# Gated attention and state-space kernel, forward and backward: head strips of 20 rows and single-bank exponentials in place of strips of 32 rows and two-bank exponentials

## The chip, the core and the metric

The kernel runs on one core of a Trainium2 chip. A core has a matmul engine (TensorE, PE in the profile, with its weight loads as PEld), a vector engine (DVE), an engine for activation functions (ACT), a general engine (GpSimd, POOL) and a queue for transfers (SyncE, SP). Sixteen DMA engines move data. Matmul results land in PSUM; the other working memory is SBUF. The metric is the device time of one execution, in microseconds: 3192.69 us before, the median of 3 runs from 3189.31 to 3194.74 us.

## The reference

Input x has 2048 rows of 576. One branch is attention with 32 heads of 18, the other a long convolution whose kernel is made from a diagonal state-space model (576 channels, 128 states); a gate mixes them. The outputs are the forward result and the gradients of all twelve trained inputs.

```python
qkv = (x @ wqkv).reshape(B, S, 3, H, Dh).transpose(2, 0, 3, 1, 4)      # S=2048, H=32, Dh=18
scores = einsum("bhqd,bhkd->bhqk", q, k) * Dh ** -0.5
o = einsum("bhqk,bhkd->bhqd", softmax(scores), v)
a = o.transpose(0, 2, 1, 3).reshape(B, S, D) @ wo
# the other branch
P = exp(dt * A * l);  K = real(einsum("dn,dnl,dn->dl", C, P, dt * Bc))    # complex A, B, C
b = causal_convolution(u, K) + u * Dskip                                 # written with FFTs
g = sigmoid((x * gate_w).sum(-1, keepdims=True))
out = g * a + (1 - g) * b
# outputs: out, and jax.vjp of it at grad_out
```

## The kernel before

The program has four parts in order: preparation, attention (forward and backward in one sweep), the convolution with its gradients, and a final part with the projections of the gradients.

**Preparation.** Loads and transposes x; makes a row-reversed copy of x; projects q, k and v per group of 7 heads, and stores each transposed, head by head, in memory. Each head has a strip of 32 rows: 18 of data, a row for the softmax bound or a constant, and 13 further rows, zeros. Four heads make 128 rows. The constant rows are written by GpSimd's queue out of a tile that uses the space of `x_pad`.

```python
QaT_d = dram.tile([NG, P, S], BF); KaT_d = ...; VaT_d = ...       # NG = 8 groups of 4 heads, P = 128
rows = [t_.rearrange("g (j w) s -> (g j) w s", w=HP) for t_ in (QaT_d, KaT_d, VaT_d)]   # HP = 32

def put_constants():
    con = s1.tile([P, 3, S // 4], BF, tag="xp")                      # the space of x_pad
    ...
    for a_ in range(4):
        for t_ in rows:
            nc.gpsimd.dma_start(t_[:, DH + 1:HP, sl], con[pt, 0:1, :].to_broadcast([H, HP - DH - 1, S // 4]))
        nc.gpsimd.dma_start(rows[1][:, DH, sl], con[pt, 2, :])        # -1
        nc.gpsimd.dma_start(rows[2][:, DH, sl], con[pt, 1, :])        # 1
...
for m, (h0, hn) in enumerate(hts):                                  # groups of 7 heads
    for which in (1, 0, 2):                                         # k, q, v
        for tb in range(NBK):
            for c, (d0, dsz) in enumerate(dch):                     # 576 = 4 x 128 + 64
                mm(ps[0:fn], lhsT=wqkv_sb[0:dsz, c, ...], rhs=xT[0:dsz, ...], ...)
            ...                                                     # eviction to stg, squares, row sums
        nc.sync.dma_start(rows[which][h0:h0 + hn, 0:DH, :], stg[0:fn, :])
...
for t in range(NT):                                                 # gradient of attention's output, through wo
    ... nc.sync.dma_start_transpose(out=d_aT, in_=d_a); nc.sync.dma_start(gyr_d[...], gy_b)   # each 4 tiles
    ... mm(psd, lhsT=d_aT[0:esz, ...], rhs=woT[0:esz, ...]); ... nc.sync.dma_start(dO_d[:, t, :], dO_t)
for r_, src_ap in enumerate((A_re, A_im, B_re, B_im, C_re, C_im)):   # parameters, two buffers
    for c, (d0, dsz) in enumerate(dch):
        nc.sync.dma_start(blk_[0:dsz, c, :], src_ap[d0:d0 + dsz, :])
    nc.sync.dma_start_transpose(out=pr_, in_=blk_)
... # powers of the poles on ACT and DVE, stored to par_d by SyncE
```

**Attention.** 32 units, each a group of 4 heads and 512 queries; a unit has 32 steps G. In a step two heads' scores (P1) are made for the forward side, two heads' scores of the transposed side (P3) and two heads' dP (P2) for a unit that runs 39 steps behind. A score matmul contracts over 32 rows of one strip, so matmuls of different strips run side by side on PE. A pair of score tiles lies in two PSUM banks, and one ACT instruction takes the exponential of both.

```python
NFILL = (0, 0, 1, 4)                       # filler matmuls by phase of four steps
def s_pair(kind):
    return apsp.tile([P, 2, KB], F32, tag="S", bufs=2)               # KB = 512
for G in range(NTOT + OFF + 24):
    ps = s_pair("P1")
    for x in range(2):
        row(ps[:, x, :], T["KaT"][:, i * P:(i + 1) * P], T["QaT", b], j0 + x)
    if G % 4 in (3, 0): ... 4 matmuls accO <- Vtok, PT                # the forward result
    ps = s_pair("P3")
    for x in range(2):
        row(ps[:, x, :], T["QaT", b][...], T["KaT"][...], jo + x)
    for x in range(2):
        row(ps_P2, T["VaT", ...], U["dOaT"], j2)                     # dP, two single banks
    ACC.append(accB(...)); fill(ACC[0], NFILL[ph])                    # one bank for dV, dQ, dK in turn
    ... # burst: 8 matmuls of dV, 8 of dQ, 16 of dK, or the fillers alone, one kind per step
    nc.scalar.activation(U["PT"][i][:, j:j + 2, :], ps, ACT.Exp)      # P1
    nc.scalar.activation(e, ps, ACT.Exp)                              # P3, e is [P, 2, KB]
    nc.vector.tensor_tensor(U["ds"][i][:, j, :], ps, U["PT"][i][:, j, :], op=A.mult)   # each of two P2
    ... # eviction of the burst on VectorE; DMA transpose of ds when 4 heads are there
```

PSUM's eight banks: two pairs of scores (4), dP (2), accO (1), accB (1). Pieces of the strips are loaded as 128-row tiles (`QaT`, `KaT`, `VaT`) and, transposed by DMA, as token tiles (`Vtok`, `Ktok`, `Qtok`). At the first steps of a unit the previous one's softmax normalisation is done: a copy of accO, four transposes on PE, then work on VectorE and GpSimd, and a DMA transpose to `dOaT`. Beside all this GpSimd computes powers of the poles (`E_d`) for the convolution.

Of the kernel before, what the change touches and what calls it, by code (L numbers as in the profile page):

```python
# [17 lines left out]
P = 128  # L18


def build(tc, aps, dbg_aps=None, stages=("s1", "attn", "post", "s4", "final")):
# [18 lines left out]
    H = 32  # L40
# [4 lines left out]
    assert DH + 2 <= HP  # L45
# [15 lines left out]
    with ExitStack() as gctx:  # L61
# [15 lines left out]
        QaT_d = dram.tile([NG, P, S], BF, name="QaT_d")  # L77
        KaT_d = dram.tile([NG, P, S], BF, name="KaT_d")
        VaT_d = dram.tile([NG, P, S], BF, name="VaT_d")
# [17 lines left out]
        dt_d = dram.tile([P, D], F32, name="dt_d")  # L97
        CB = 32
# [14 lines left out]
        with ExitStack() as ctx:  # L113
# [11 lines left out]
            x_pad = s1.tile([P, NT, DPAD], BF, tag="xp", name="x_pad")  # L125
            nc.gpsimd.memset(x_pad[:, :, D:DPAD], 0.0)
            wqkv_sb = s1.tile([P, DC, F], BF, name="wqkv_sb")
            xT = s1.tile([P, NT, DC, P], BF, name="xT")
# [20 lines left out]
            rows = [t_.rearrange("g (j w) s -> (g j) w s", w=HP) for t_ in (QaT_d, KaT_d, VaT_d)]  # L149
            xb_v = xb_d.rearrange("b (k r) w -> b k r w", r=XR)  # L150

            def put_constants():

                con = s1.tile([P, 3, S // 4], BF, tag="xp", name="con")
                for q_, v_ in enumerate((0.0, 1.0, -1.0)):
                    nc.gpsimd.memset(con[:, q_, :], v_)
                for a_ in range(4):
                    sl = slice(a_ * S // 4, (a_ + 1) * S // 4)
                    pt = slice(a_ * H, (a_ + 1) * H)
                    for t_ in rows:  # L160
                        nc.gpsimd.dma_start(t_[:, DH + 1:HP, sl], con[pt, 0:1, :].to_broadcast([H, HP - DH - 1, S // 4]))
                    nc.gpsimd.dma_start(rows[1][:, DH, sl], con[pt, 2, :])
                    nc.gpsimd.dma_start(rows[2][:, DH, sl], con[pt, 1, :])

            hsel = s1.tile([P, HT], BF, name="hsel")
            nc.gpsimd.memset(hsel, 1.0)
            nc.gpsimd.affine_select(out=hsel, in_=hsel, compare_op=A.is_ge, fill=0.0,
                                    base=0, pattern=[[-DH, HT]], channel_multiplier=1)
            nc.gpsimd.affine_select(out=hsel, in_=hsel, compare_op=A.is_ge, fill=0.0,
                                    base=DH - 1, pattern=[[DH, HT]], channel_multiplier=-1)  # L170

            for t in range(NT):
                xr_t = work.tile([P, D], BF, tag="xr_t4", bufs=4, name="xr_t4")
                for u in range(2):
                    psr = psB.tile([P, 512], F32, tag="dO", bufs=2, name="psr")
                    mm(psr[:, 0:DH2], lhsT=J_bf, rhs=x_pad[:, t, u * DH2:(u + 1) * DH2])
                    if u == 0:
                        nc.vector.tensor_copy(xr_t[:, 0:DH2], psr[:, 0:DH2])
                    else:
                        nc.scalar.copy(xr_t[:, DH2:D], psr[:, 0:DH2])  # L180
                nc.sync.dma_start(xr_d[:, t, :], xr_t)
# [9 lines left out]
            put_constants()  # L191
            kmx = s1.tile([HT, len(hts), NBK], F32, name="kmx")
            kmxg = s1.tile([HT, len(hts)], F32, name="kmxg")
            for m, (h0, hn) in enumerate(hts):
                fn = hn * DH
                for which in (1, 0, 2):
# [3 lines left out]
                    for tb in range(NBK):  # L200
                        ps = psA.tile([P, TB, P], F32, tag="proj", bufs=4, name="ps_proj")
                        for c, (d0, dsz) in enumerate(dch):
                            mm(ps[0:fn], lhsT=wqkv_sb[0:dsz, c, which * D + h0 * DH:which * D + h0 * DH + fn],
                               rhs=xT[0:dsz, tb * TB:(tb + 1) * TB, c, :], start=(c == 0), stop=(c == DC - 1))
# [12 lines left out]
                        ps2 = psB.tile([HT, TB * P], F32, tag="ps2", name="ps2")  # L217
                        mm(ps2[0:hn], lhsT=hsel[0:fn, 0:hn], rhs=sq[0:fn])
# [15 lines left out]
            for t in range(NT):  # L234
# [11 lines left out]
                for u, (f0, fsz) in enumerate(HALF):  # L246
                    psd = psB.tile([P, 512], F32, tag="dO", bufs=2, name="ps_dO")
                    for c, (e0, esz) in enumerate(dch):
                        mm(psd[:, 0:fsz], lhsT=d_aT[0:esz, t % TB, c, :], rhs=woT[0:esz, c, f0:f0 + fsz],
                           start=(c == 0), stop=(c == DC - 1))  # L250
# [12 lines left out]
            for r_, src_ap in enumerate((A_re, A_im, B_re, B_im, C_re, C_im)):  # L263
                blk_ = work.tile([P, DC, N], BF, tag="pblk", name="pblk")
                nc.vector.memset(blk_[:, DC - 1, :], 0.0)
                for c, (d0, dsz) in enumerate(dch):
                    nc.sync.dma_start(blk_[0:dsz, c, :], src_ap[d0:d0 + dsz, :])
# [64 lines left out]
        if "attn" in stages:  # L332
# [4 lines left out]
            NFILL = (0, 0, 1, 4)  # L337
            with ExitStack() as ctx:
# [15 lines left out]
                PB = {"QaT": 3, "VaT": 4, "Vtok": 5, "Ktok": 4, "Qtok": 2}  # L354

                def load_full(g):
                    t_ = ga.tile([P, S], BF, tag="KaT", bufs=2, name="KaT_g")
                    nc.sync.dma_start(t_, KaT_d[g])
                    grp_t.setdefault(g, {})["KaT"] = t_

                def load_piece(nm, g, m):
                    src = {"QaT": QaT_d, "VaT": VaT_d, "Vtok": VaT_d, "Ktok": KaT_d, "Qtok": QaT_d}[nm][g][:, m * KB:(m + 1) * KB]
                    if nm in ("QaT", "VaT"):
                        t_ = ga.tile([P, KB], BF, tag=nm, bufs=PB[nm], name=nm + "_g")
                        nc.sync.dma_start(t_, src)
                    else:
                        t_ = ga.tile([P, TPQ, 4, HP], BF, tag=nm, bufs=PB[nm], name=nm + "_g")
                        nc.sync.dma_start_transpose(out=t_.rearrange("p t h w -> p t (h w)"), in_=src)
# [64 lines left out]
                def row(ps, l, r, j):  # L433
                    r0 = HP * j
                    mm(ps, lhsT=l[r0:r0 + DA], rhs=r[r0:r0 + DA], tile_position=(r0, 0))

                def s_pair(kind):
                    return apsp.tile([P, 2, KB], F32, tag="S", bufs=2, name="ps_" + kind)
# [955 lines left out]
```

## Time and profile before

| | PE | DVE | ACT | POOL |
|---|---|---|---|---|
| busy, us | 2580.9 | 2389.7 | 2394.6 | 1803.1 |
| share of the span of 3191.0 us | 81% | 75% | 75% | 57% |

A share of the whole span mixes stages, so the table of stretches (busy time of each engine between two times) is read with it. A line of a group in the profile gives the line of the program, the engine, output and inputs with shapes, the number of instructions, then busy time in us and the mean of one in ns, then the idle time of the engine just ahead of them and what ended it. In the views by time, the first number is the start, the second the duration, and "x4" means four instructions merged in one line. A busy time counts overlapping instructions once; the durations of neighbours can overlap, so what an engine needs for one is read from start to start.

### The profile page before, as it was taken

The numbers are of one execution on the slowest core, as the hardware profiler recorded it, in microseconds if no ns is written. First come the engines' busy times: TensorE is split into PE (matmuls) and PEld (weight loads), VectorE is DVE, ScalarE is ACT, GpSimd is POOL, SyncE is SP. The second block draws the span as 40 slices with busy tenths as digits, with TensorE's granted clock in tenths as the row PEclk, the third lists the DMA queues.
The fourth block names the chain that finished last, engine by engine and source line by source line (L and its number), as shares of the span: only waits on it lengthen the run. The fifth ranks groups of instructions, "written<-read, shape, count | busy, mean of one in ns | idle before, by whom it ended". The sixth has DMA issues, their size and how long they took to land. (4 is left out here: it accounts for less than half of the span.)

```text
span 3191.0 us, 69289 instructions
## 1 busy us (share of the span) xinstructions
PE 2580.9 (81%) x26530; PEld 1162.4 (36%) x26530; DVE 2389.7 (75%) x4309; ACT 2394.6 (75%) x2760; POOL 1803.1 (57%) x3376
## 2 busy tenths in 40 slices
PE   6668888888888888888888888888856877885498
PEld 2222222222222222222222222222215777775255
DVE  4245787888788788888788878888855888888533
ACT  3239898998899899899899989998846676773010
POOL 1019888888888888888888888887010000000000
PEclk9778999999999899999899999999977888887799
DMA  8966999999999999999999999998898787862995
GB/s 224 152 166 113 182 174 186 176 172 175 182 167 171 186 165 180 185 178 174 177 186 171 178 187 171 173 184 164 148 186 219 207 207 200 213 176 65 278 241 131
DMA packets 1536483, 572.12 MB, mean 179 GB/s; under 512 B 1428511, under 2 KB 1503650, under 8 KB 1526934
## 3 DMA queue, kind: packets, MB, share of 16 engines
q1 hardware_dynamic: 1514278, 509.95, 81.9%
q0 software_dynamic: 21872, 57.74, 7.4%
q8 instruction: 207, 3.39, 0.4%
q14 instruction: 126, 1.03, 0.1%
HBM read 153.55 MB, written 102.83 MB: 80 GB/s over the span
## 5 line engine op out<-in xcount | busy, mean ns | idle before, releaser
L768 DVE TENSOR_TENSOR ds<-ps_P,PT 128x512 bf16<-128x512 f32 x2048 | 1316.0, 684 | 305.0 <-ACT eb L763 143.3
L758 ACT ACTIVATE PT<-ps_P 128x1024 bf16<-128x1024 f32 x1024 | 1064.6, 1042 | 171.4 <-PE ps_P L30 155.9
L763 ACT ACTIVATE eb<-ps_P 128x1024 bf16<-128x1024 f32 x1024 | 1072.7, 1048 | 28.4 <-PE ps_P L30 26.9
L542 POOL TENSOR_TENSOR et<-eG,eT 128x256 f32<-128x256 f32 x1152 | 700.7, 629 | 35.2
L30 PE MATMUL ps_P<-KaT_g,QaT_g 32*128 32x512 bf16 x2048 | 411.9, 391 | 102.8 <-ACT eb L763 98.2
L30 PE MATMUL ps_P<-dOaT,VaT_g 32*128 32x512 bf16 x2048 | 449.5, 395 | 23.1 <-DMA dOaT<-dOa 14.7
L542 POOL TENSOR_TENSOR Eo<-et,et 128x256 bf16<-128x256 f32 x576 | 418.7, 727 | 43.1
L30 PE MATMUL ps_P<-QaT_g,KaT_g 32*128 32x512 bf16 x2048 | 416.7, 404 | 20.6 <-DMA Vtok_g<-VaT_d 12.3
L1056 POOL TENSOR_TENSOR SS<-m 128x96 f32<-128x96 f32 x18 | 7.9, 440 | 560.4 <-ACT m L1054 560.4
L30 PE MATMUL accF<-ident_bf,J_bf 128*128 128x512 bf16 x1044 | 295.9, 409 | 1.6 <-DVE gb L527 1.4
L30 PEld LDWEIGHTS <-QaT_g 32*128 32x128 bf16 x2048 | 166.8, 91 | 340.0 <-issue 336.5
L30 PEld LDWEIGHTS <-KaT_g 32*128 32x128 bf16 x2048 | 104.9, 91 | 416.6 <-issue 404.2
L30 PE MATMUL accQ<-ds,Ktok_g 128*32 128x512 bf16 x2048 | 161.6, 391 | 88.9 <-DVE dvacc L479 63.9
L30 PEld LDWEIGHTS <-J_bf 128*128 128x128 bf16 x1364 | 118.5, 100 | 284.2 <-issue 224.3
L30 PE MATMUL accO<-PT,Vtok_g 128*32 128x512 bf16 x2048 | 212.6, 401 | 0.1
L30 PE MATMUL accK<-dsT,Qtok_g 128*32 128x256 bf16 x4096 | 175.5, 296 | 10.9 <-DMA dsT<-ds 10.8
L30 PE MATMUL accV<-eb,dOa 128*32 128x512 bf16 x2048 | 159.9, 389 | 0.6 <-DVE Ob L400 0.5
L30 PE MATMUL accK<-ident_bf,J_bf 128*128 128x512 bf16 x256 | 100.6, 393 | 69.8 <-DVE dqa L499 55.1
L30 PEld LDWEIGHTS <-Qtok_g 128*32 128x32 bf16 x4096 | 90.6, 100 | 161.2 <-issue 141.9
L912 ACT COPY E1e<-etp 128x1024 bf16<-128x1024 bf16 x144 | 135.8, 1042 | 13.6 <-PE etp L911 13.5
L30 PE MATMUL yp<-Rw,E1n 128*128 128x30 bf16 x1152 | 67.9, 232 | 88.9 <-DVE Rw L975 73.5
L30 PEld LDWEIGHTS <-E1n 128*128 128x128 bf16 x2304 | 96.8, 109 | 107.9 <-issue 107.4
(243 smaller groups left out, 3724.8 us busy)
## 6 DMA issues: line engine op xcount, KB each, us to landing
E_d<-Eo POOLq DMA_DIRECT2D x144, 256.0 KB, 4.0
E1n<-E_d SPq DMA_DIRECT2D x36, 1024.0 KB
xs<-xb_d SPq DMA_DIRECT2D x18, 1024.0 KB
T0w<-Kp_d SPq DMA_DIRECT2D x18, 1024.0 KB
Md_d<-mst SPq DMA_DIRECT2D x36, 288.0 KB
dsT<-ds SPq DMA_TRANSPOSE x512
dqkv_d<-dtk POOLq DMA_DIRECT2D x96, 72.0 KB, 4.2
dq_u<-dqkv_d SPq DMA_DIRECT2D x4, 1728.0 KB
```

The lines of the kernel that those rows point to most:

```text
L30: return nc.tensor.matmul(out, lhsT=lhsT, rhs=rhs, start=start, stop=stop, **kw)
L542: nc.gpsimd.tensor_tensor(out, a, b, op=op)
L758: nc.scalar.activation(U["PT"][i][:, j:j + 2, :], ps, ACT.Exp)
L763: nc.scalar.activation(e, ps, ACT.Exp)
L768: nc.vector.tensor_tensor(U["ds"][i][:, j, :], ps, U["PT"][i][:, j, :], op=A.mult)
L912: nc.scalar.copy(E_[:, 4 * q:4 * q + 4], pt_)
L1056: nc.gpsimd.tensor_tensor(o_[:, :, 0], m4[:, :, 0], m4[:, :, 3], op=A.subtract)
```

## The change

It has two sides. In preparation, a head's strip in memory has 20 rows (18 of data and up to two constant rows), all of q, k and v in one tensor; there are no zero rows in it. Where attention reads 32 rows of a strip, 12 of them belong to the next head; the other operand has zeros there (Q tiles are cleared once and loaded with 19 rows per head, and the padded rows of dO are zero). Token tiles are transposed from 80 rows in place of 128. The parameter tensors are loaded at the start by GpSimd's queue, in two transfers each, and the constant rows follow them, from a tile of their own. Every contraction is over 128 rows, with zeros in the weights beyond row 576, and the row sums of squares give 128 output rows. The reversed copy of x is stored four tiles at a time. It is meant to move less data before attention and to keep the transfer queue free.

In attention, the exponentials are 512 wide over single banks, four of them, where they were 1024 wide over pairs; the six score and dP matmuls of a step come one kind after another, ahead of accO; and two phases have a filler matmul more.

```diff
-        QaT_d = dram.tile([NG, P, S], BF, name="QaT_d")
-        KaT_d = dram.tile([NG, P, S], BF, name="KaT_d")
-        VaT_d = dram.tile([NG, P, S], BF, name="VaT_d")
+        QKV_d = dram.tile([3 * H * HS + HP - HS, S], BF, name="QKV_d")      # HS = DH + 2 = 20
...
+            nc.vector.memset(wqkv_sb[D - (DC - 1) * P:P, DC - 1, :], 0.0)
...
-            def put_constants(): ...
+            con = s1.tile([P, 2, S // 8], BF, name="con")
+            for r_, src_ap in enumerate((A_re, A_im, B_re, B_im, C_re, C_im)):
+                ...
+                nc.gpsimd.dma_start(blk_[:, 0:nf, :], src_ap[0:nf * P, :].rearrange("(c p) n -> p c n", p=P))
+                nc.gpsimd.dma_start(blk_[0:D - nf * P, nf, :], src_ap[nf * P:D, :])
+            for a_ in range(4):
+                for w_ in range(3):
+                    for y_ in range(DH + (w_ == 0), HS):
+                        nc.gpsimd.dma_start(rows[w_][:, y_, sl]..., con[...].to_broadcast([H, 2, S // 8]))
...
-                nc.sync.dma_start(xr_d[:, t, :], xr_t)
+                if t % TB == TB - 1:
+                    nc.sync.dma_start(xr_d[:, t + 1 - TB:t + 1, :], xr_t)
...
-                            mm(ps[0:fn], lhsT=wqkv_sb[0:dsz, c, ...], rhs=xT[0:dsz, ...], ...)
+                            mm(ps[0:fn], lhsT=wqkv_sb[:, c, ...], rhs=xT[:, ...], ...)
...
-            NFILL = (0, 0, 1, 4)
+            NFILL = (1, 1, 1, 4)
...
+                            for j in range(4):
+                                r0 = (4 * g + j) * HS
+                                nc.sync.dma_start(t_[HP * j:HP * j + DH + 1, :], QKV_d[r0:r0 + DH + 1, m * KB:(m + 1) * KB])
...
-                        nc.sync.dma_start_transpose(out=t_.rearrange("p t h w -> p t (h w)"), in_=src)
+                        nc.sync.dma_start_transpose(out=t_[:, 0:TPQ * 4 * HS]..., in_=QKV_d[... 80 rows, 512 columns])
...
-                def s_pair(kind):
-                    return apsp.tile([P, 2, KB], F32, tag="S", bufs=2, name="ps_" + kind)
+                    tg, nb = ("dP", 2) if kind == "P2" else ("S", 4)
+                    ps = apsp.tile([P, KB], F32, tag=tg, bufs=nb, name="ps_" + kind)
...
+                    for x in range(2):
+                        if r1: rows.append(("P1", ..., row("P1", ..., j0 + x)))
+                        if r2: rows.append(("P3", ..., row("P3", ..., jo)))
+                               rows.append(("P2", ..., row("P2", ..., j2)))
...                    # accO now comes after these six
-                            nc.scalar.activation(U["PT"][i][:, j:j + 2, :], ps, ACT.Exp)
+                            nc.scalar.activation(U["PT"][i][:, j, :], ps, ACT.Exp)
...
-                            e = work.tile([P, 2, KB], BF, tag="eb", bufs=6, name="eb")
+                            e = work.tile([P, KB], BF, tag="eb", bufs=12, name="eb")
                             nc.scalar.activation(e, ps, ACT.Exp)
```

## The prediction

> **What bounds the kernel now.** I read the table of stretches first, for the stages; then the groups by line; then the order of time of two stretches.
>
> ```profile
> 80.00:120.00 40.00, 13.05 (x29) 4.04 (x28) 5.24 (x13) 2.36 (x4) 4.10 (x7) 0.55 1.18 150
> ...
> 800.00:1200.00 400.00, 342.39 (x3356) 112.38 (x3355) 329.55 (x562) 361.81 (x387) 345.31 (x642) 0.94 0.98 175
> 1200.00:1600.00 400.00, 346.82 (x3397) 114.10 (x3395) 333.26 (x569) 366.37 (x392) 351.58 (x653) 0.94 0.99 179
> ```
>
> The columns are PE, weight loads, DVE, ACT, POOL, clock, DMA share, GB/s. Three stages follow: preparation to about 230 us (first exponential), attention to 2352 us (last exponential), the convolution and final part after that, 839 us, which the diff leaves alone. Attention decides: ACT is busy over 90% of it. A step has one exponential of each kind, so 1570 ACT instructions from 400 to 2000 us make 785 steps of 2.04 us; a unit of 32 steps takes 65.2 us, and there are 32 units.
>
> ```profile
> L768 DVE TENSOR_TENSOR ds<-ps_P,PT 128x512 bf16<-128x512 f32 x2048 | 1316.0, 684 | 305.0 <-ACT eb L763 143.3
> L758 ACT ACTIVATE PT<-ps_P 128x1024 bf16<-128x1024 f32 x1024 | 1064.6, 1042 | 171.4 <-PE ps_P L30 155.9
> L763 ACT ACTIVATE eb<-ps_P 128x1024 bf16<-128x1024 f32 x1024 | 1072.7, 1048 | 28.4 <-PE ps_P L30 26.9
> ```
>
> Here the reader sees that ACT, when it waits at all, waits for the score matmuls. Next, how one exponential follows another:
>
> ```profile
> 1202.33 1.02 ACT L758 ACTIVATE PT<-ps_P 128x1024 bf16<-128x1024 f32 x1
> 1203.25 1.02 ACT L763 ACTIVATE eb<-ps_P 128x1024 bf16<-128x1024 f32 x1
> 1204.16 1.03 ACT L758 ACTIVATE PT<-ps_P 128x1024 bf16<-128x1024 f32 x1
> ...
> 1208.68 1.09 ACT L763 ACTIVATE eb<-ps_P 128x1024 bf16<-128x1024 f32 x1
> 1209.86 1.02 ACT L758 ACTIVATE PT<-ps_P 128x1024 bf16<-128x1024 f32 x1
> ```
>
> The durations (1.04) overlap; start to start is 0.905 us, so a step costs ACT 1.81 us. From 1202.33 to 1209.86 four steps take 7.53 us: 4 x 1.81 and one hole of 0.28 (1208.68 to 1209.86 instead of 0.905). A unit at this pace is 60.2 us; the other 5 us of its 65.2 lie in the first eight steps, where VectorE also does the softmax normalisation.
>
> In preparation, SyncE's queue hardly waits, it is filled by issuing:
>
> ```profile
> 71.17 23.36 SPq L243 DMA_TRANSPOSE d_aT<-d_a  x1
> ...
> 97.95 21.98 SPq L243 DMA_TRANSPOSE d_aT<-d_a  x1
> ```
>
> The same issue takes 3 to 5 us at 182 and 195 us. At 64 to 106 us GpSimd's writes of constant rows run, up to 19 us each to land.
>
> **What the skill says.** PSUM — Partial Sum Buffer, "The four PSUM rules", gives a bank 512 fp32 columns; so two heads of 512 take two banks, and before and after alike four banks hold scores: two pairs or four singles. ScalarE: Activation LUTs, "Rules for kernel authors", budgets a constant part and a part per element for an ACTIVATE; the trace agrees in kind (1024 wide 0.905 us, 512 wide 0.48 us, next part), with a smaller constant than the page's 0.3 us when instructions follow closely. DMA: Bandwidth & Descriptors, "Issuing engines are not separate DMA queues", says DMAs of all issuers share 16 engines and interleave; the two stretched transposes beside GpSimd's writes fit it. TensorE: Matmul & The Clock Gate, "What's actually happening", says idling halves the clock; here score matmuls of 0.39 us read 0.61 in the disturbed start of a unit.
>
> **Part 1: exponentials of 512.** A 512-wide f32 activation from PSUM exists in the convolution stage:
>
> ```profile
> 2508.18 2.07 ACT L937 ACTIVATE UV<-uvp 128x512 bf16<-128x512 f32 x4
> 2510.10 1.11 ACT L1014 CAST yd<-yp 128x512 bf16<-128x512 f32 x2
> ```
>
> Four in (2510.10 - 2508.18) = 1.92 us, 0.48 each (0.477 where the starts can be read more finely). A step has four of them: 1.908 us, 0.098 more than 1.81. Over 1024 steps that alone is +100 us.
>
> **Part 2: what remains of the holes.** The hole before is a loop: ACT ends a pair; 0.19 us later PE starts the next pair in that bank; then fill and burst; then the next score pair; 0.43 us after its start ACT can begin. In the steps with the dK burst the fill waited for VectorE's eviction of the single accumulator, and the loop took about 2.1 us against 1.81. The new order puts all six score matmuls of a step first, then accO, fill, burst. Start-to-start gaps from the same stretch: score to accO 0.33, accO to next 0.33, fill to burst 0.30, dV burst to score 0.59, dK burst 0.55. The new loop, from the end of the last exponential of a step: 0.19 + 0.33 + 0.33 + 0.30 + 0.59 + 0.43 = 2.17 us, where four single banks allow 1.908: a hole of 0.26. The next step also has accO and a burst, but its loop began before the hole, so it finds the time already given; the dK step is 0.19 + 0.33 + 0.30 + 0.55 + 0.43 = 1.80, the four-fill step 1.91. VectorE has at most 1.8 us in a step (two products at 0.60, one eviction) and follows. So four steps are 4 x 1.908 + 0.26 = 7.89 us, a unit 63.1 against 60.2: +2.9 us, over 32 units +93 us. I chose the full loop; without its new fill (0.30) there would be no hole and the sum +28 us (4 x 1.908 = 7.63, so 61.1 a unit).
>
> **Part 3: unit starts.** They cost 5 us now. Slower steady steps give VectorE 0.1 us more room in each, the two added fills keep the clock up, but a blocked P2 matmul now stands in front of half the step's scores, with 0.95 us of exponentials in hand instead of 1.81. I set these against each other and keep 5 us, minus about 0.4 for the room: -13 us. Attention: +93 - 13 = +80 us.
>
> **Part 4: preparation.** Constant rows shrink from 13 to 1 or 2 per head and tensor: 5.1 MB to about 0.7 MB, issued at the start and no longer after x_pad is free. The two transposes fall from 23 and 22 us to about 5 each: -35 us. SyncE also loses 30 parameter loads (about 0.5 us each, -15 us) and 12 of 16 xr stores, which get larger. At the start 1.5 MB more compete with x and wqkv: +4 us. The dO stage of some 35 us at the end (176 to 216 us) stays, and so does the load of the first group (222 to 230). Sum about -50 us, first exponential near 180 us. Full 128-row contractions do not shorten it: in the trace 64-row and 128-row projection matmuls both follow each other at about 0.27 us.
>
> **Part 5: strips of 20 rows.** Token transposes shrink from 128 to 80 columns, Q pieces become four loads of 19 rows. In attention waits for these transfers are small (12.3 us for Vtok, 14.7 us for dOaT over the whole kernel), and the dsT transposes, 512 of four times the size of a token piece, remain. SyncE waits over 850 us for VectorE there, so 96 further issues fit. I count 0.
>
> Sum: 3193 + 80 - 50 = 3223, rounded to 3225 us.
>
> **Rivals.** (a) ACT stays nearly full with single banks: the finer hand-over closes the holes and eases unit starts; +28 or less in attention, so 3140 to 3170 us. For it: buffers are freed every 0.48 us; in favour too are the fills kept at (1, 1, 1, 4), which an author would hardly keep if they hurt. Against it: the loop above. (b) Unit starts get worse, because PE stands behind VectorE with fewer scores ahead: 3 us more per unit, about 3320 us. For it: the ACT wait on PE of 155.9 us already comes mainly from there. (c) DMA sets attention's pace, with its share of 0.98: then shorter strips give back a few per cent and the exponentials' width is free, about 3120 us. Against it: waits for DMA in attention are under 50 us, and the steady steps repeat at exactly ACT's pace. (d) Preparation is bound by PE, whose stretch 120 to 160 us is 38 of 40 us busy: then only the stall of 80 to 120 goes, -30 us in place of -50.
>
> **Range and chances.** Attention +80 with about 45 either way, preparation -50 with 15: low 3155, high 3290. The 2% limits are 3129 and 3257. Faster by over 2% needs (c), or (a) with a much larger gain in preparation: 0.10. Slower needs a little worse than my loop, or (b): 0.30. Within 2%: 0.60.
>
> **What would show it.** Right: first exponential at 170 to 195 us, the d_aT transposes without a 20 us issue, exponentials 0.477 us apart, one hole of about 0.26 us in four steps, a unit near 67.7 us, and the part after attention still near 839 us. Wrong: four steady steps at 7.63 us (rival a) or over 8.1 us (two holes), a unit start costing over 7 us (rival b), first exponential above 200 us (rival d).

## The result and the profile after

| | before | after |
|---|---|---|
| time, us (median, range) | 3193.72 (3189.31 to 3209.72) | 3238.12 (3235.70 to 3246.48) |
| ratio to before, 95% interval | | 1.0134 (1.0095 to 1.0174) |
| first exponential of attention, us | 230.2 | 197.3 |
| attention, first to last exponential, us | 2121.8 | 2201.4 |
| convolution and final part, us | 839.0 | 837.6 |
| four steady steps of attention, us | 7.53 | 7.98 |
| unit of 32 steps, us: the three ordinary units of a group | 63.7 | 64.6 |
| unit in which the group changes, us | 70.8 | 78.1 |

The stages are from the profiled execution of each kernel (spans 3191.0 and 3236.3 us). Preparation gave 33 us, attention took 80, the rest stayed. A steady step is the median, over units, of the time from one P1 exponential to the next at the same place of the unit. One unit of the four of a group is longer than the others, the second: there the backward side, which runs 39 steps behind, goes over to the new group of heads, the finished gradients of the old group are transposed, and K of the group after is loaded. I call it the group change. All stage times below are of one profiled execution each; the ratios are of timed runs. Sixty timed runs of the kernel before on one chip lay between 3182 and 3223 us, so a difference of two stages of this length is good to some 10 us; step and unit times, which are medians and means of many, are steadier.

The table of stretches of the changed kernel, with columns as before (PE, weight loads, DVE, ACT, POOL, clock, DMA share, GB/s):

```profile
80.00:120.00 40.00, 27.58 (x98) 14.65 (x98) 17.77 (x45) 13.62 (x23) 0.00 (x0) 0.82 0.84 166
...
1200.00:1600.00 400.00, 373.10 (x3385) 117.30 (x3388) 326.17 (x551) 378.21 (x758) 336.54 (x628) 0.98 1.00 168
```

In the first line the hole of preparation is partly filled: 27.58 us of PE in 40 where there were 13.05. In the other, of attention, ACT is busier than before (378 of 400 against 366) and yet gets less done: 758 instructions of half the width, where 392 of the full width fitted. The groups by line:

```profile
L791 ACT ACTIVATE PT<-ps_P 128x512 bf16<-128x512 f32 x2048 | 1275.1, 627 | 136.5 <-PE ps_P L30 124.4
L795 ACT ACTIVATE eb<-ps_P 128x512 bf16<-128x512 f32 x2048 | 1290.7, 632 | 25.9 <-PE ps_P L30 25.8
```

The exponentials' busy time grew from 1064.6 and 1072.7 us to 1275.1 and 1290.7, but their durations overlap, and this growth is not the loss: that is read from the order of time. ACT's waits on PE before the P1 exponentials are rarer and longer: 124.4 us in 78 waits, the longest 10.2, where there were 155.9 us in 201 waits, the longest 5.1.

A steady stretch by time. It is cut to the loop that the prediction worked out and to the exponentials of its end:

```profile
1149.97 0.68 ACT L791 ACTIVATE PT<-ps_P 128x512 bf16<-128x512 f32 x1
...
1150.21 0.37 PE L30 MATMUL ps_P<-KaT_g,QaT_g 32*128 32x512 bf16 x1
...
1150.53 0.40 PE L30 MATMUL accO<-PT,Vtok_g 128*32 128x512 bf16 x4
...
1150.86 0.39 PE L30 MATMUL accV<-ident_bf,J_bf 128*128 128x512 bf16 x1
...
1151.18 0.61 PE L30 MATMUL accV<-eb,dOa 128*32 128x512 bf16 x8
1151.41 0.71 ACT L795 ACTIVATE eb<-ps_P 128x512 bf16<-128x512 f32 x1
...
1151.73 0.38 PE L30 MATMUL ps_P<-KaT_g,QaT_g 32*128 32x512 bf16 x1
...
1152.15 0.60 ACT L791 ACTIVATE PT<-ps_P 128x512 bf16<-128x512 f32 x1
```

Counted from 1149.97, where ACT turns from one exponential to the next, PE starts the last score of the step 0.24 us later, then accO (0.32), the filler (0.33), the dV burst (0.32), the next score (0.55), and ACT can begin after 0.42: 2.18 us. Four starts 0.477 us apart would take 1.91 us, so there is one hole, 1151.41 to 1152.15 in place of 0.48. This is the predicted loop.

By their ends the exponentials tell something more. In a train without a hole the starts are 0.477 us apart, but each lasts a little longer than the one before it (0.68 to 0.71 us above), and the ends are 0.490 us apart; for the pairs of before it is 0.904 and 0.916. Start to start, the reading that was proposed further up and used in the prediction, is thus too short for a full engine. What ACT can do is set by the ends: 16 x 0.490 = 7.84 us for four steps where the kernel before needed 8 x 0.916 = 7.33. The hole adds 0.14 us (the ends at 1152.12 and 1152.75 are 0.63 apart), before it added some 0.20 (from the end at 1209.77 to that at 1210.88, in place of 0.916). So 7.98 = 7.84 + 0.14, and 7.53 = 7.33 + 0.20: the whole loss of the steady steps is the width, and the holes are a little smaller than before.

### The profile page after: what moved, and what is told of

Read it like the earlier page. It is cut to its first block, busy times and chain, and to the rows that moved or that the text cites. A ratio compares the mean times of both kernels' runs of the same rounds, so it can differ in the third digit from the quotient of the medians.

```text
span 3236.3 us, 71505 instructions
## 1 busy us (share of the span) xinstructions
PE 2795.2 (86%) x27042; PEld 1217.4 (38%) x27042; DVE 2411.5 (75%) x4310; ACT 2520.0 (78%) x4807; POOL 1819.8 (56%) x3407
## 4 chain that ended last, share of the span: by engine, by line
ACT 30%; PE 26%; DVE 19%; DMA 11%; POOL 7%; issue 5%; SPq 2%; DVEq 0%; POOLq 0%; ACTq 0%
ACT PT L791 15%; ACT eb L795 13%; PE ps_P L30 7%; PE accV L30 5%; POOL et L583 3%; DMA dsT<-ds 3%; DVE tz L982 3%; PE accO L30 3%; DVE ds L800 2%; DVE tz L985 2%; DVE HG L986 2%; PE ps_dx L30 2%; PE accF L30 2%; PE accK L30 1%; POOL Eo L583 1%
## 5 line engine op out<-in xcount | busy, mean ns | idle before, releaser
L791 ACT ACTIVATE PT<-ps_P 128x512 bf16<-128x512 f32 x2048 | 1275.1, 627 | 136.5 <-PE ps_P L30 124.4
L795 ACT ACTIVATE eb<-ps_P 128x512 bf16<-128x512 f32 x2048 | 1290.7, 632 | 25.9 <-PE ps_P L30 25.8
L30 PE MATMUL ps_P<-dOaT,VaT_g 32*128 32x512 bf16 x2048 | 786.5, 392 | 48.0 <-DMA dOaT<-dOa 30.9
L30 PE MATMUL ps_P<-KaT_g,QaT_g 32*128 32x512 bf16 x2048 | 749.6, 386 | 37.0
L30 PE MATMUL ps_P<-QaT_g,KaT_g 32*128 32x512 bf16 x2048 | 648.3, 394 | 16.6 <-DMA QaT_g<-QKV_d 14.4
L30 PEld LDWEIGHTS <-VaT_g 32*128 32x128 bf16 x2048 | 178.8, 91 | 376.8 <-issue 343.4
L30 PEld LDWEIGHTS <-J_bf 128*128 128x128 bf16 x1876 | 163.1, 98 | 361.2 <-issue 287.0
L30 PE MATMUL accF<-ident_bf,J_bf 128*128 128x512 bf16 x1044 | 277.8, 390 | 3.1 <-DVE gb L568 3.1
L520 DVE TENSOR_TENSOR dvacc<-dvacc,accV 128x512 f32<-128x512 f32 x192 | 131.7, 686 | 74.0 <-PE accV L30 73.6
L30 PE MATMUL accK<-dsT,Qtok_g 128*32 128x256 bf16 x4096 | 163.7, 281 | 16.4 <-DMA dsT<-ds 10.3
L540 DVE SCALAR_TENSOR_TENSOR dqa<-accQ,dqa 128x512 f32<-128x512 f32 x192 | 131.9, 687 | 12.7 <-PE accQ L30 4.1
```

The costliest lines, as they stand in the source:

```text
L30: return nc.tensor.matmul(out, lhsT=lhsT, rhs=rhs, start=start, stop=stop, **kw)
L520: nc.vector.tensor_tensor(o_, a_, acc, op=A.add)
L540: nc.vector.scalar_tensor_tensor(o_, acc, c_scale, a_, op0=A.mult, op1=A.add)
L791: nc.scalar.activation(U["PT"][i][:, j, :], ps, ACT.Exp)
```

## The experiments

Three ideas are tested. Theory 1, for the whole: the width of the exponentials, with the fillers, costs attention its steady steps, and the short strips cost it the long group changes; so the two can be had apart. Its rival puts the long stalls down to the new order of the score matmuls, and makes the strips free. A second idea, for the group change: the strips' transfers run on few DMA engines, and what comes beside or behind them is late. Theory 3, for the same: SyncE's queue is full there, and each further issue, or each longer one, lengthens the unit. Ratios are to runs of the kernel before on the same chip.

| run | ratio, 95% interval | first exponential | attention | four steady steps | group change |
|---|---|---|---|---|---|
| e1: new preparation, pairs | 1.0055 (1.0037 to 1.0073) | 197.8 | 2178.1 | 7.53 | 79.6 |
| e2: old preparation, singles | 1.0046 (1.0034 to 1.0057) | 230.6 | 2145.6 | 7.98 | 69.9 |
| e3: changed, fillers 0, 0, 1, 4 | 1.0061 (1.0046 to 1.0076) | 196.2 | 2177.0 | 7.84 | 77.7 |
| e4: changed, strips by head | 1.0033 (1.0012 to 1.0055) | 192.5 | 2189.3 | 7.98 | 76.3 |
| e5: before, K in 16 transfers | 1.0080 (1.0055 to 1.0106) | 240.4 | 2159.2 | 7.53 | 76.1 |
| e6: changed, strips on GpSimd's queue | 1.0151 (1.0124 to 1.0179) | 199.8 | 2216.6 | 7.98 | 70.8 |
| e7: changed, fillers 0, 0, 1, 2 | 1.0039 (1.0025 to 1.0054) | 200.0 | 2178.2 | 7.84 | 80.4 |
| e8: changed, parameters later on SyncE | 1.0104 (1.0073 to 1.0136) | 195.7 | 2204.5 | 7.98 | 78.5 |
| e9: before, new start of preparation | 1.0076 (1.0047 to 1.0105) | 254.8 | 2143.5 | 7.53 | 72.3 |
| e10: before, early parameters | 0.9973 (0.9956 to 0.9990) | 219.7 | 2132.3 | 7.53 | 71.7 |
| e11: before, early constant rows | 1.0046 (1.0029 to 1.0063) | 244.9 | 2130.8 | 7.53 | 72.4 |
| e12: e1 with K padded in place of Q | 0.9988 (0.9971 to 1.0005) | 199.2 | 2168.8 | 7.53 | 76.5 |

### The two sides apart: e1 and e2

e1 is the changed kernel with the exponentials of before; e2 is the kernel before with those of the change.

```diff
# e1, against the changed kernel
-    tg, nb = ("dP", 2) if kind == "P2" else ("S", 4)
+    return apsp.tile([P, 2, KB], F32, tag="S", bufs=2, name="ps_" + kind)      # and the old order of a step
-    NFILL = (1, 1, 1, 4)
+    NFILL = (0, 0, 1, 4)
# e2, against the kernel before: the same lines the other way round
```

> The kernel after with the attention order of before put back (pairs of banks, exponentials 1024 wide, fillers 0,0,1,4); preparation and the 20-row strips stay. Theory 1 (the long stalls of the units in which the group of heads changes come from the new strip loads, which run on few DMA engines): the stalls come along, so 3193 - 33 (preparation) + 55 = about 3215 us, and units with a group change stay about 7 us above those of before. Rival (the stalls come from the single banks, because PE stands behind a late P2 with fewer scores ahead): no such stalls, about 3160 us.

> The kernel before with the attention of after alone (single banks, exponentials 512 wide, six score matmuls first, fillers 1,1,1,4); preparation and strips of 32 rows as before. Theory 1 (stalls from the strip loads): only the slower steady steps are left, 32 units x 0.9 us, so about 3222 us and ordinary group changes. Rival (stalls from the single banks): +80 us as in the kernel after, about 3273 us.

e1 has the old steady steps (7.53 us) and keeps the long group changes (79.6 us). e2 has the new steady steps (7.98) and no long group change (69.9). So the strips lengthen it, not the order of the matmuls. From the two, attention's 79.6 us come apart with almost nothing left: the exponentials and fillers alone make it 2145.6 - 2121.8 = 23.8 us longer, the strips alone 2178.1 - 2121.8 = 56.3 us. And all of preparation's gain is on the side of the strips (197.8 against 230.6). The sum is so even partly by chance: in the timed runs the two sides cost 0.55 and 0.46%, together 1.01%, and the whole change 1.34% (0.95 to 1.74).

### The fillers: e3 and e7

```diff
-            NFILL = (1, 1, 1, 4)
+            NFILL = (0, 0, 1, 4)        # e3
+            NFILL = (0, 0, 1, 2)        # e7
```

> The kernel after with the fillers of before (0,0,1,4). Theory (the loop of the prediction): without the filler the loop is 0.30 us shorter, 1.87 us against 1.908, so the hole closes; four steady steps 7.63 in place of 7.98 us, 32 x 8 x 0.35 = -89 us, about 3150 us. Rival (the fillers keep TensorE's clock up, or the hole has another cause): four steps stay at 7.9 us or more and the time at 3238 us or above.

Four steps fell from 7.98 to 7.84 us, not to 7.63. By starts, the hole behind the dV burst closed and another seems to open in the step with four fillers. By time, in e3:

```profile
1131.19 0.78 ACT L791 ACTIVATE PT<-ps_P 128x512 bf16<-128x512 f32 x1
...
1131.53 0.37 PE L30 MATMUL ps_P<-KaT_g,QaT_g 32*128 32x512 bf16 x1
...
1131.85 1.04 PE L30 MATMUL accF<-ident_bf,J_bf 128*128 128x512 bf16 x4
...
1132.63 0.80 ACT L795 ACTIVATE eb<-ps_P 128x512 bf16<-128x512 f32 x1
...
1132.83 0.39 PE L30 MATMUL ps_P<-KaT_g,QaT_g 32*128 32x512 bf16 x1
...
1133.24 0.69 ACT L791 ACTIVATE PT<-ps_P 128x512 bf16<-128x512 f32 x1
```

From 1131.19, where ACT turns to the next exponential, it is 0.34 us to PE's score, then 0.32 to the fillers, 0.98 to the next score and 0.41 to ACT, in all 2.05 us, more than 1.91. But the exponential of 1132.63 lasts until 1133.43, past the start at 1133.24: ACT never stands here. The late start only takes up the lead that the starts had gained on the ends. e7 cuts that step too:

> The kernel after with fillers 0,0,1,2. In the run with 0,0,1,4 the hole had moved to the step with four fillers, whose loop measures 2.05 us from its parts. Theory (loops of PE's order): two fillers fewer take 0.43 us off that loop, no loop is over 1.908 us, four steady steps become 7.63 to 7.70 us (7.84 with 0,0,1,4, 7.98 with 1,1,1,4), about -35 us against the run with 0,0,1,4. Rival (TensorE's clock needs the fillers): granted clock in attention falls below 0.9 and the steps get longer.

The steady steps stayed at 7.84, though now the second of four is the long one by starts (2.07 us). Two fillers fewer did not let the clock drop (0.94 in attention). Both runs have the pace that the ends give, 16 x 0.490 = 7.84 us, and in steps 12 to 28 of the ordinary units ACT is idle, from one exponential's end to the next one's start, for 0.00 us of four steps in e3 and e7, and for 0.03 in the changed kernel. So without the filler the hole is gone and ACT is full; what was expected, 7.63, was below what ACT does with exponentials of this width. The theory of e7, that another loop held e3 back, is not borne out: shortening that loop changed nothing.

### The group change: e4, e5, e6, e12

The order of time at a group change in the changed kernel, cut to SyncE's queue (SPq), the VectorE instruction that ends the softmax normalisation, and the waits of PE and ACT that follow:

```profile
1047.09 0.52 DVE L451 TENSOR_SCALAR dOa<-dl 128x16 bf16<-128x16 f32 x1
...
1048.38 2.00 SPq L806 DMA_TRANSPOSE dsT<-ds  x1
...
1050.46 1.57 SPq L408 DMA_TRANSPOSE Ktok_g<-QKV_d  x1
...
1052.13 3.96 SPq L806 DMA_TRANSPOSE dsT<-ds  x1
...
1056.18 0.54 SPq L452 DMA_DIRECT2D O_d<-Ob  x1
1056.82 0.45 SPq L417 DMA_DIRECT2D dO_b<-dO_d  x1
1057.36 1.20 SPq L454 DMA_TRANSPOSE dOaT<-dOa  x1
...
1060.01 0.60 PE L30 MATMUL ps_P<-dOaT,VaT_g 32*128 32x512 bf16 x1 [6.71 <-DMA dOaT<-dOa]
...
1061.08 0.60 ACT L791 ACTIVATE PT<-ps_P 128x512 bf16<-128x512 f32 x1 [6.57 <-PE ps_P L30]
```

SyncE goes from one issue to the next with some 0.1 us between them. VectorE has finished dOa, which the next dP matmuls need, at 1047.61; its transpose is issued at 1057.36, behind all that stood in the queue. PE stands 6.71 us for it, and ACT, without scores, 6.57. Some 10 us later comes the load of K, after and then before:

```profile
1068.82 0.58 SPq L390 DMA_DIRECT2D KaT_g<-QKV_d  x1
1069.51 1.21 SPq L463 DMA_TRANSPOSE gT<-gb  x1
1070.81 7.46 SPq L806 DMA_TRANSPOSE dsT<-ds  x1
```

```profile
1067.61 0.42 SPq L358 DMA_DIRECT2D KaT_g<-KaT_d  x1
1068.12 4.57 SPq L774 DMA_TRANSPOSE dsT<-ds  x1
```

The bytes of the K tile are the same, 128 packets of 4096 bytes. They took 6.9 us after, on average 3.4 in flight at once, and 3.5 us before, with 9.1 in flight; the dsT issue beside them took 7.46 us. A second stall follows from it:

```profile
1084.55 1.29 DVE L800 TENSOR_TENSOR ds<-ps_P,PT 128x512 bf16<-128x512 f32 x2 [7.27 <-DMA dsT<-ds]
...
1085.30 0.58 PE L30 MATMUL ps_P<-dOaT,VaT_g 32*128 32x512 bf16 x1 [5.28 <-DVE ds L800]
...
1086.34 0.60 ACT L791 ACTIVATE PT<-ps_P 128x512 bf16<-128x512 f32 x1 [5.21 <-PE ps_P L30]
```

VectorE has no free ds tile (there are four) until a dsT transpose has landed, PE no free dP bank, ACT no score. VectorE's waits of this kind sum to 47.8 us in the changed kernel (longest 8.3) and to 14.6 in e2 (longest 2.9), which has the same attention code; PE's for dOaT to 30.9 and 15.4. The last group change loads no further K, and there the second stall is absent: its steps 12 to 20 take 16.0 us in the changed kernel, in the six others 23.3 on average. The Trainium skill, DMA: Bandwidth & Descriptors, "Why a DMA increments its semaphore by 16 and not by 1", says that a transfer is spread over the largest number of engines, up to 16, that divides the slowest dimension on both sides. Worked out from this rule, as an estimate: the K strip is read as 4 x 32 x 2048, which gives 4 engines; a plain tile of 128 rows gives 16; 19 rows of Q give one, 20 rows ten. K's packets in flight agree in kind (3.4 against 9.1).

e4 reads K and V as four transfers of 32 rows each and Q in 20 rows (row 19 of Q's strip is written as zero for that):

```diff
-                    nc.sync.dma_start(t_, strip(1, g, 0, S))
+                    for j in range(4):
+                        r0 = HR + (4 * g + j) * HS
+                        nc.sync.dma_start(t_[HP * j:HP * (j + 1), :], QKV_d[r0:r0 + HP, :])      # V the same way
...
-   nc.sync.dma_start(t_[HP * j:HP * j + DH + 1, :], QKV_d[r0:r0 + DH + 1, m * KB:(m + 1) * KB])
+   nc.sync.dma_start(t_[HP * j:HP * j + HS, :], QKV_d[r0:r0 + HS, m * KB:(m + 1) * KB])
```

> The kernel after with every strip load made to spread over more DMA engines: K and V as four loads of 32 rows, one per head, and Q as four loads of 20 rows in place of 19 (row 19 of Q's strip is written as zero). Theory 1: the long stalls at group changes go, -55 us, about 3185 us; the 4 KB packets of a K load end within about 3.5 us as in the kernel before. Rival (stalls from the single banks, or from the number of issues in SyncE's queue, which grows): 3238 us or more.

The dsT issues did get shorter, 3.25 to 2.81 us each and 55.2 to 48.2 us in a group change, but K and V now took 6.7 us of SyncE's time there instead of 1.7, and the unit fell only from 78.1 to 76.3. That pointed to SyncE itself. Its issues and its issue time in a group change, the unit's length, and two stretches of it, in us (means of seven group changes; the two stalls shown above lie in the two stretches):

| | issues | SyncE issuing | of it dsT | unit | first eight steps | steps 12 to 20 |
|---|---|---|---|---|---|---|
| before | 32.6 | 67.3 | 49.3 | 70.8 | 22.0 | 16.4 |
| e2 | 31.0 | 65.5 | 48.5 | 69.9 | 19.6 | 16.6 |
| after | 35.6 | 72.9 | 55.2 | 78.1 | 23.0 | 22.3 |
| e1 | 36.0 | 74.3 | 55.6 | 79.6 | 25.3 | 23.2 |
| e4 | 44.4 | 71.9 | 48.2 | 76.3 | 24.2 | 17.5 |
| e5 | 45.6 | 72.6 | 47.2 | 76.1 | 22.1 | 18.2 |
| e12 | 35.6 | 70.8 | 51.9 | 76.5 | 24.7 | 18.6 |

In the unit ahead of the group change SyncE of the changed kernel issues for 60.4 of 64.4 us, in the other two for 48.5 and 55.0 of about 64.6; in the group change all but some 5 us of a longer unit. Over these seven kernels the unit's length follows the issue time with 3.5 to 5.7 us between them. But what lengthened it in the changed kernel is hardly the count: three more issues than before, those of Q, take 1.0 us, while the 17 dsT issues take 5.9 us more. Most of that is one issue, the dsT beside the K load: 7.9 us on average, before 4.3, where the other dsT issues of attention take 2.8 and 2.6. In e4 those beside K are short (2.9 us) and steps 12 to 20 are nearly those of before; the nine more issues cost most of that again, in the other stretches.

For the count alone, the queue was made longer in the kernel before, at the same bytes:

```diff
-                    nc.sync.dma_start(t_, KaT_d[g])
+                    for r0 in range(0, P, 16):
+                        for c0 in (0, S // 2):
+                            nc.sync.dma_start(t_[r0:r0 + 16, c0:c0 + S // 2], KaT_d[g, r0:r0 + 16, c0:c0 + S // 2])
```

> The kernel before with one edit: a group's K tile is loaded in 16 transfers of 16 rows by half the columns in place of one transfer, same bytes. Theory 3 (in the unit with the group change SyncE's queue is full, so its issue time sets the unit's length): 15 further issues of about 0.45 us make each of the eight group-change units some 6 to 7 us longer, in all about +50 us (ratio 1.016), other units unchanged. Rival (the strip loads hurt by the way they spread over the DMA engines, not by issue time): these loads spread over 16 engines and move the same bytes, so under +10 us.

The group change went from 70.8 to 76.1 us with nothing else changed in it, so theory 3 holds as far as it goes: a fuller queue is enough for a loss of this size. But it lies elsewhere in the unit than that of the changed kernel, mostly behind step 20; the first eight steps stayed, and steps 12 to 20 grew by 1.8 us, not 5.8. The other units stayed (64.3, 64.2, 63.1). The first exponential came 10 us later too, as the first group's K is also in 16 parts. The profiled execution was 43 us longer than that of before, the timed runs by 26 (0.8%), less than I had put down.

e6 takes the loads of strips off SyncE:

```diff
-nc.sync.dma_start(t_, strip(...))          # K, V, and the four of Q
+nc.gpsimd.dma_start(t_, strip(...))
```

> The kernel after with the K, Q and V strip loads issued from GpSimd's queue in place of SyncE's; transposes and all else stay with SyncE. Theory 3 (SyncE's issue time sets the group-change unit): four Q, two V and one K issue leave the queue, and the token and ds transposes no longer queue behind them; the unit falls from 78 to about 70 us, in all -60 us, about 3180 us. Rival (it is the transfers themselves): nothing, 3238 us. A risk on the same line: GpSimd's own work is delayed, which would show in the first steps of every unit.

The group change fell to 70.8 us, that of the kernel before. But the unit after it rose from 64.5 to 72.0 us; the two together take what they took in the changed kernel (142.8 against 142.6 us). The list of waits shows on which engine: VectorE's wait for GpSimd's product in the softmax normalisation. In e6, then in the changed kernel (total us, times, longest):

```profile
DVE dl L450 <- POOL prod L444: 78.7, 15, 8.2
```

```profile
DVE dl L450 <- POOL prod L444: 8.8, 5, 3.7
```

GpSimd has its own stream of work, and what it issues delays the normalisation that every unit start needs. So the wait was moved, not removed.

e12, on top of e1, takes nine issues per group off SyncE: the zeros lie in the K tiles (cleared once, loaded as four times 20 rows per group), and Q comes in one transfer of 4 x 32 rows per piece.

```diff
+                kat = []                                     # two K tiles, cleared once
...
-                            for j in range(4):
-                                nc.sync.dma_start(t_[HP * j:HP * j + DH + 1, :], QKV_d[r0:r0 + DH + 1, ...])
+                        nc.sync.dma_start(t_, strip(w, g, m * KB, KB))             # Q as V
...
-                    nc.sync.dma_start(t_, strip(1, g, 0, S))
+                    for j in range(4):
+                        nc.sync.dma_start(t_[HP * j:HP * j + HS, :], QKV_d[r0:r0 + HS, :])
```

> The changed kernel's preparation and short strips with the exponentials of the kernel before (pairs, fills 0, 0, 1, 4), and the padding moved from the Q tiles to the K tiles: K tiles are cleared once and loaded with four transfers of 20 rows per group, Q pieces come as one transfer of 32 overlapping rows per head. That takes 9 issues per group off SyncE's queue (12 Q, less 3 more for K) and replaces the slow whole-group K transfer by four of 20 rows. If SyncE's issue time sets the length of the group-change unit, that unit falls from 79.6 us (the same kernel with Q padded) to 72 to 75 us and the total from 3224 to 3170 to 3185 us, a ratio of 0.99 to 0.995. If it is set by the bytes or by the transposes of 80 rows, the unit stays at 78 us or more and the total near 3220 us.

The group change fell from 79.6 to 76.5 us, about half of what theory 3 alone asked for, and the kernel from 0.55% above before to level with it. SyncE's issue time went down by 3.5 us and the unit by 3.1. The count of issues in the group change did not fall, though (36.0 and 35.6: what Q lost there K gained); the dsT issues fell, from 55.6 to 51.9 us, those beside K from 8.0 to 3.4, and steps 12 to 20 from 23.2 to 18.6 us.

So the 7.3 us come apart by place. Nearly all the growth of steps 12 to 20 (5.8 us) hangs on the K load and the dsT issue that it lengthens: it is absent where no K is loaded, and e4 and e12, which load K in four wider transfers, lose most of it. The width and the splitting are not told apart by these two; that the width matters is seen in e1 and before, each with one K transfer of the same bytes (8.0 and 4.3 us for the dsT beside it). The other part is in the first eight steps, where dOaT waits in the queue: 23.0 us against 19.6 in e2, 25.3 in e1 against 22.0 before. Neither e4 nor e12 brought it back, and which of the strips' transfers causes it stays open.

### Preparation: e8, e9, e10, e11

In the changed kernel the transposes of x at the start and the two that the prediction named:

```profile
8.80 27.57 SPq L138 DMA_TRANSPOSE xT<-x_pad  x4
...
70.65 8.74 SPq L257 DMA_TRANSPOSE d_aT<-d_a  x1
83.94 11.63 SPq L257 DMA_TRANSPOSE d_aT<-d_a  x1
```

The d_aT issues fell to 8.74 and 11.63 us, but the four for x rose from 17.13 to 27.57, beside the loads that GpSimd now issues. PE did 12.73 us of work in the first 40 where it did 22.73. e8 gives the parameter loads to SyncE, behind the transposes of wo:

```diff
-                nc.gpsimd.dma_start(blk_[:, 0:nf, :], ...)             # ahead of the constant rows
+                nc.sync.dma_start(blk_[:, 0:nf, :], ...)               # behind woT
```

> The kernel after with the parameter loads issued by SyncE after the transposes of wo, and no longer by GpSimd at the start. Theory (at the start they compete with x and delay its transposes, which take 27.6 us of issue in place of 17.1): the xT transposes fall back towards 17 us and the first exponential comes about 5 to 8 us earlier, near 190 us; the whole -6 us. Rival (the constant rows delay the transposes, or another wait takes over): the transposes stay at 25 us or more, or the first exponential stays at 197 us.

```profile
8.83 18.42 SPq L138 DMA_TRANSPOSE xT<-x_pad  x4
```

The transposes of x are back at 18.42 us, and yet the first exponential came only 1.7 us earlier. The twelve parameter loads, from 45.58 to 52.72 us, now stand ahead of the stores of the reversed x; VectorE waits 13.58 us for such a store (`DVE L192 ... [13.58 <-DMA xr_d<-xr_t]` at 55.86), and PE 10.50 us at the same place, where it waited 4.64 in the changed kernel. e9, e10 and e11 put the new start into the kernel before, whole and in its two halves; the strips stay at 32 rows and the attention is that of before.

```diff
# e10: parameters by GpSimd at the start, xr_d in stores of four tiles
+                nc.gpsimd.dma_start(blk_[:, 0:nf, :], src_ap[0:nf * P, :].rearrange("(c p) n -> p c n", p=P))
+                nc.gpsimd.dma_start(blk_[0:D - nf * P, nf, :], src_ap[nf * P:D, :])
# e11: constant and zero rows at the start, from a tile of their own
-                con = s1.tile([P, 3, S // 4], BF, tag="xp", name="con")
+                con = s1.tile([P, 3, S // 4], BF, name="con")
# e9: both (con half as wide, twice as many writes)
```

> The kernel before with its strips of 32 rows and its attention unchanged, and only the start of preparation taken from the changed kernel: the parameters are loaded at the start by GpSimd's queue in two transfers each, the constant and zero rows follow them out of a tile of their own, the reversed copy of x is stored four tiles at a time. Theory: what preparation gained (first exponential at 230 before, 197 in the changed kernel) comes from when these transfers are issued, and the short strips only cost time in attention. Then the first exponential comes at 197 to 207 us (the zero rows are still 4.3 MB), group-change units stay at 70.8 us, the total is near 3165 us, a ratio of 0.99. Rival: the gain comes from the bytes that the short strips save; then the early writes of the zero rows stretch the loads and transposes at the start, the first exponential stays above 222 us, and the total is 3185 us or more.

> The kernel before with only the early parameter loads and the larger stores of the reversed x; the constant rows are written as before, out of the space of x. If SyncE's issues (30 parameter loads, 12 stores) are what held preparation, the first exponential comes near 210 us; if the stretched transposes of the attention gradient are (23.4 and 22.0 us beside the constant rows), it comes at 225 us or later, with these two issues still near 20 us.

> The kernel before with only the constant and zero rows written at the start out of a tile of their own; parameters and stores as before. If the stretched transposes held preparation, they fall to about 9 and 12 us or less and the first exponential comes near 210 us; if SyncE's own issues do, it comes at 222 us or later.

My theory for e9 fell. e11 came at 244.9 us, past the 222 that were put down for SyncE's own issues, but that was not the reason: its d_aT issues were short, and the transposes of x were longer than anywhere. With the zero rows written early the first exponential of e9 came at 254.8 us, 25 later than before, though the d_aT issues were short (two as one entry of 6.82 us). The transposes of x paid for it, in e9 and then in e11:

```profile
9.39 36.63 SPq L136 DMA_TRANSPOSE xT<-x_pad  x4
```

```profile
9.20 43.64 SPq L136 DMA_TRANSPOSE xT<-x_pad  x4
```

So the stretch of transposes beside the writes of constant rows is not avoided by moving the writes: with 5.1 MB of them it moves to whichever transposes run beside them, and at the start it costs more. With the short strips, whose writes are some 0.7 MB, the early place went with the short d_aT issues and 197.3 us; short strips with late writes were not run. e10, parameters and larger stores alone, brings the first exponential to 219.7 us, 10.5 of the 33, between the two cases that were expected; its d_aT issues are still 24.09 and 14.63 us. It is the one run that beats both kernels, that of before by 0.27% (0.10 to 0.44).

## Why the prediction was right, and where it was not

The total was close (3225 against 3238 us), but by luck: errors of opposite sign in its terms nearly cancelled.

- **Part 1** (exponentials 0.477 us apart, +100 us over the steps) is right in kind and too small. The starts are 0.48 apart, but the cost is read from the ends: 4 x 0.490 - 2 x 0.916 = 0.13 us a step, +131 us. The instructions that Part 1 read, of the convolution, do end 0.48 apart; the exponentials do not.
- **Part 2** holds in its mechanism: one hole in four steps, behind accO, filler and dV burst, a loop of 2.18 us against 2.17. By ends the hole is 0.14 us, not 0.26, as the starts had a lead to lose. Four steps were 7.98 against 7.89 us, that is 3.6 us a unit where I had 2.9 (8 x 0.45 against 8 x 0.36). The version without the filler, which I put at 7.63, is wrong: e3 and e7 measured 7.84, a full ACT.
- **Part 3** is the most mis-sized term of the exponentials' side. "I keep 5 us, minus about 0.4": the unit starts fell by far more. The exponentials' side alone cost attention 23.8 us (e2), while the steady loss is 3.6 x 32 = 115; so the unit starts gave some 91 us, not 13. In the ordinary units, 64.6 - 8 x 7.98 = 0.8 us are left beyond the steady pace, where there were 3.4. A slower pace, which leaves VectorE more time, is not the whole of it: the first eight steps of an ordinary unit take 16.7 us where they took 18.4, less in absolute time. What in the new order serves the start of a unit better was not tried. The 5 us were also an average of 3.4 us in ordinary units and 10.6 in group changes.
- **Part 4**, -50, was -33, and the first exponential, at 197.3 us, lies just past the 170 to 195 that were named. The d_aT transposes fell by 25 us, not 35, and "1.5 MB more compete: +4 us" was too small: the transposes of x took 10 us longer. e10 shows the parameters and stores at 10.5 us (I had 15 for the loads alone). That full 128-row contractions bring nothing was not tried alone. Rival (d) had the size nearly right, but its reason is not seen: from 120 to 160 us PE was busy for 31.79 of 40 us.
- **Part 5**, "I count 0", is the step that failed: the strips cost attention 56.3 us (e1), and it lies in the group changes (70.8 to 79.6 us there, 78.1 in the changed kernel). I had averaged SyncE's free time over attention ("waits over 850 us") and found room for 96 issues. The room is in the other units; in the group change there were 3.5 us left of 70.8. The further issues themselves take 1.0 us there; what filled the queue is the dsT issues, 5.9 us longer, above all the one beside K. I had taken the short strips for cheaper transfers by their bytes, without asking over how many engines their shape spreads. The waits that I called small were a sign of it: of the seven for dOaT in the kernel before (14.7 us), six lie in group changes, while the 12.3 us for Vtok are one wait ahead of attention.

So attention was +80 as predicted, but as +24 and +56, not +80 and 0. Of the rivals, (a) did not come: the hole closed only without the filler (e3, e7), and then ACT itself needs 7.84 us for four steps, not 7.63. (b) is nearest to what the strips did, PE standing at a unit start and later in the unit, but in the end for a transfer and not for VectorE's work. (c) is refuted: with the short strips alone (e1) attention became longer, and the steady pace followed ACT.

## What to carry to other kernels

Look at the issuing queue stage by stage, as at an engine: an average that leaves it a quarter of its time says nothing of the one unit in which it is full, and there a longer queue is paid for (15 more issues, 5.3 us more in e5). Before reshaping a tensor to save bytes, count the issues and see over how many DMA engines the new shape spreads; 32 overlapping rows of four heads moved the same tile in twice the time, and the transpose issued beside it took nearly twice as long too. Where durations overlap, read a pace from the ends as well as from the starts, over a stretch long enough: the starts ran ahead here by 0.013 us an exponential, and a "hole" between starts can be one in which the engine never stood. And when a change has two sides, run each alone first: here each was of another size than thought.

## What the runs showed of the hardware

- ACT's exponentials lengthen in an unbroken train: their starts stay 0.477 us apart, their ends 0.490, so in the changed kernel they go from 0.60 us after a hole to 0.71 ahead of the next, in e3 to 0.81, in e7 to 0.91. In the kernel before the pairs go from 1.02 to 1.09 us, with 0.904 and 0.916 between starts and ends. The bank that PE waits for is free at the end: PE starts 0.05 us behind it in the changed kernel (1150.16 to 1150.21), 0.06 in e3.
- The issue of a DMA transpose occupies SyncE for a time that depends on the transfers beside it: 1.2 us at the least, 2.3 to 3.3 us on average for dsT by unit of attention, 7.9 us for the one beside the changed kernel's K load, 43.64 us for the four of x in e11.
- The load of K as 4 x 32 rows took 6.9 us, as 128 rows 3.5, for the same bytes.
